# Output stores cut into multiples of 16 rows, and the last block's tiles evicted and stored one by one

## The chip, the cores and the metric

The kernel runs on one core of one Trainium2 chip. The metric is the device time of one execution in microseconds (us); the median of several runs is compared. The engines are TensorE (PE, with its weight loads PEld), VectorE (DVE), ScalarE (ACT), GpSimd (POOL) and SyncE (SP). SP does no arithmetic here: it issues nearly all DMAs, one after another in program order.

## The reference, cut to what matters

```python
X = np.fft.fft(x, axis=1)                 # x: 8 x 3008 x 256
X = np.fft.fft(X, axis=2)
h = X.real.reshape(24064, 256)
gate = np.maximum(h @ w_gate, 0.0)        # 256 x 1536
val = h @ w_val
out = (gate * val) @ w_out                # 1536 x 256, out: 24064 x 256 float32
```

A real part of a two-dimensional Fourier transform of each of eight batches, then a gated two-layer network on its rows.

## The kernel before, in words

The eight batches are eight blocks `b`. The transform along the sequence is a matmul with sine and cosine tables; the transform along the channels is folded into the network's weights (WA, WB, WM). Because the transform is symmetric, one set of columns gives two output rows: the rows that belong to +k and to −k. Block 0 is worked in four segments of 376 or 377 columns, blocks 1 to 7 in three thirds of 512, 512 and 481 columns. For each third, twelve tiles `fi` of 128 hidden channels are made: gate and value are computed in PSUM, multiplied by VectorE (L620), and stand in bf16 tiles `h` of 2n columns, the plus rows first and the mirrored minus rows behind them.

The output matmuls of a third (L511, `todo_out`) run while the next third's hidden tiles are made, some of them after each step. `out_steps` lays them out. It cuts the 2n columns of `h` into units of 128; each unit takes 12 matmuls of 128 x 256 into a PSUM tile `o`, and two units share one tile (two tiles `o` exist). When a pair is done, `fin` copies it with ScalarE (L518) into an SBUF tile `os` (four of them) and SP stores it. The 66 columns of a 481-column third that don't fill a unit are copied by a DMA into `LB` (L615); when 128 of them have come together they form a unit of their own, and in the last block the last 78 form one.

Neighbouring columns of a unit are output rows two apart, but a unit can cross from one run of rows to another. So `fin` walks over the rows and issues one store for each run (L528):

```python
while r[p] is not None and e < len(r) and r[e] == r[e - 1] + 2:
    e += 1
```

A unit of 128 rows thus becomes one store of 128 rows, or two such as 104 and 24, 97 and 31, 89 and 38. A row is 256 float32, 1 KB. DMAs on SP take turns on eight completion semaphores, so each also waits for the landing of the eighth before it.

Evictions are not issued at once but put into a list (`evict`), from which one is taken per tile while the blocks overlap (`paired`). After the last block's tiles nothing overlaps any more: the code calls `finish(pending)` and then `run(todo_out, len(todo_out))`, which issues the 96 output matmuls of the last third and empties the list. That last third has seven units of 128 (units 0 to 6) and the 78-row unit, in four pairs: rows 104 + 24 and 128; 128 and 97 + 31; 128 and 128; 89 + 38 and 12 + 66. For the last pair, whose second unit is shorter than 128, each unit is copied by itself (L521).

The order of instructions on each engine is the program's (a manual schedule); the tile pools insert the waits.

Of the kernel before, what the change touches and what calls it, by code (L numbers as in the profile page):

```python
# [13 lines left out]
ALU = mybir.AluOpType  # L14
# [13 lines left out]
def dram(ap, offset, pattern):  # L28
    return bass.AP(ap.tensor, offset, [list(p) for p in pattern])
# [3 lines left out]
def kernel(  # L33
# [8 lines left out]
    nc = tc.nc  # L42
    B, S, D = x.shape
    DF = moe_w_gate.shape[1]
    NF = DF // 128
# [15 lines left out]
    def single(name, shape, dt=F32, pool=const):  # L61
        return pool.tile(shape, dt, name=name, tag=name)
# [145 lines left out]
    for r, want in enumerate((0, H // 2)):  # L208
        have = H - 1 - 256 - 120 - r * H // 2
        nc.vector.scalar_tensor_tensor(gf[:, r:r + 1], in0=z[:], scalar=float(want - have), in1=gf[:, r:r + 1],  # L210
                                       op0=ALU.mult, op1=ALU.add)
# [48 lines left out]
    for n, c in enumerate(order):  # L260
        q, m = (single(f"{s}{c}", [128, NJ], pool=st_) for s in "qm")
# [41 lines left out]
    for t in range(3):  # L303
        p, ts = slice(0, ROWS[1][t]), slice(t, t + 1)
# [56 lines left out]
    def flush():  # L361
        for todo in (evict, sums):
            while todo:
                todo.pop(0)()
# [106 lines left out]
    def row_of(col, plus):  # L471

        seg, j = (3, col - 3 * NJ) if col >= 3 * NJ else divmod(col, NJ)
        if seg == 0:
            return 2 * j + 1 if plus else S - 2 * j - 1
        if seg == 1:
            return H + 2 * j + 1 if plus else H - 2 * j - 1
        if seg == 2:
            return H + 2 * j if plus else (H - 2 * j if j else None)
        return 2 * j if plus else (S - 2 * j if j else None)  # L480

    def out_steps(b, block, hs):

        nonlocal left_done
        c0, n = block

        r = [row_of(c0 + i, True) for i in range(n)] + [row_of(c0 + n - 1 - i, False) for i in range(n)]
        r = [None if v is None else b * S + v for v in r]
        units, whole = [], n // 64
        if n < 481:  # L490
            whole = 6
        for k in range(whole):
            h0 = min(128 * k, 2 * n - 128)
            units.append((lambda f, h0=h0: hs[f][:, h0:h0 + 128], [None] * (128 * k - h0) + r[128 * k:h0 + 128]))
        if n == 481:
            left_rows.extend(r[128 * whole:])
            while len(left_rows) - left_done >= 128 or b == B - 1 and left_done < len(left_rows):
                o = left_done
                k = min(128, len(left_rows) - o)
                units.append((lambda f, o=o, k=k: LB[:, f, o % 256:o % 256 + k], left_rows[o:o + k]))  # L500
                left_done += k
        steps = []
        for k in range(0, len(units), 2):
            st = {}
            some = units[k:k + 2]
            for q, (lhs, r) in enumerate(some):
                for f in range(NF):
                    def mm(st=st, q=q, f=f, lhs=lhs, m=len(r)):
                        if "p" not in st:
                            st["p"] = psO.tile([128, 2, D], F32, name="o", tag="o")  # L510
                        nc.tensor.matmul(st["p"][0:m, q, :], lhsT=lhs(f), rhs=wo[:, f, :],  # L511
                                         start=(f == 0), stop=(f == NF - 1))
                    steps.append(mm)

            def fin(st=st, some=some):
                os_ = rp.tile([128, 2, D], F32, name="os", tag="os", bufs=4)
                if len(some[-1][1]) == 128:
                    nc.scalar.copy(os_[:, 0:len(some)], st["p"][:, 0:len(some)])  # L518
                for q, (_, r) in enumerate(some):
                    if len(some[-1][1]) < 128:  # L520
                        nc.scalar.copy(os_[0:len(r), q], st["p"][0:len(r), q])  # L521
                    p = 0
                    while p < len(r):
                        e = p + 1
                        while r[p] is not None and e < len(r) and r[e] == r[e - 1] + 2:
                            e += 1
                        if r[p] is not None:
                            nc.sync.dma_start(out=dram(out, r[p] * D, [[2 * D, e - p], [1, D]]), in_=os_[p:e, q, :])  # L528
                        p = e
            last = steps[-1]  # L530

            def last_and_fin(last=last, fin=fin):
                last()
                evict.append(fin)
            steps[-1] = last_and_fin
        return steps
# [21 lines left out]
    todo_out, todo_dft, todo_fold = [], [], []  # L558
# [3 lines left out]
    def run(todo, n):  # L562
        for _ in range(min(n, len(todo))):
            todo.pop(0)()
        if not paired:
            flush()
# [61 lines left out]
    def finish(st):  # L628
        mirror(st["v"], st, 1)
        second(st)  # L630
# [10 lines left out]
    def tile_of(block, fi, uvc):  # L641
        c0, n = block
        cols = slice(c0, c0 + n)
        return {"n": n, "fi": fi, "f": slice(fi * 128, (fi + 1) * 128), "us": uvc[0][:, cols], "vs": uvc[1][:, cols], "c": uvc[2][:, cols]}
# [127 lines left out]
    for b in range(B):  # L772
# [4 lines left out]
        for blk, block in enumerate(blocks):  # L777
# [35 lines left out]
            if (b, blk) == (0, 0):  # L813
                for fi in range(NF):
                    st = tile_of(block, fi, (U, V, CB))
# [4 lines left out]
            elif not paired:  # L820
                for fi in range(NF):
                    st = tile_of(block, fi, (U, V, CB))
# [21 lines left out]
            if blk == len(blocks) - 1 or (b, blk) == (0, 1):  # L844
                run(todo_dft, len(todo_dft))
            todo_out = out_steps(b, block, hs)
        if b:
            run_fold(99)
# [1 line left out]
            U, V, CB = Un, Vn, CBn  # L850
    paired = False
    finish(pending)
    run(todo_out, len(todo_out))
# [1 line left out]
_INS = ['x', 'moe_w_gate', 'moe_w_val', 'moe_w_out']  # L855
_OUTS = [((24064, 256), 'float32')]
# [25 lines left out]
```

## Time and profile before

| | us |
|---|---|
| median of 3 runs | 652.28 (651.86 to 652.97) |
| profiled execution, whole time | 651.86 |
| profiled execution, span from first to last instruction | 650.1 |
| mean granted TensorE clock | 0.993 of full speed |
| last hidden-tile matmul begins | 628.50 |
| last output matmul and last eviction end | 639.35 and 640.07 |
| last store issued | 642.82 |

The span is what the profile shows between the first and the last instruction; the whole time holds 1.76 us more. In the lines of the profile, a name such as L511 is the kernel's line, "SPq" is an instruction of SP's queue (a DMA's issue, not its transfer), and "x4" a merged group of four. The view of windows gives for each stretch the busy time of PE, PEld, DVE, ACT and POOL with the number of instructions, then the granted TensorE clock, the mean busy share of the 16 DMA engines and the GB/s they moved. The view of waits gives: who waited, for whom, us in total, times, longest.

### The profile page before, as it was taken

The numbers are of one execution on the slowest core, as the hardware profiler recorded it, in microseconds if no ns is written. First come the engines' busy times: TensorE is split into PE (matmuls) and PEld (weight loads), VectorE is DVE, ScalarE is ACT, GpSimd is POOL, SyncE is SP. The second block draws the span as 40 slices with busy tenths as digits, with TensorE's granted clock in tenths as the row PEclk, the third lists the DMA queues.
The fourth block names the chain that finished last, engine by engine and source line by source line (L and its number), as shares of the span: only waits on it lengthen the run. The fifth ranks groups of instructions, "written<-read, shape, count | busy, mean of one in ns | idle before, by whom it ended". The sixth has DMA issues, their size and how long they took to land.

```text
span 650.1 us, 12382 instructions
## 1 busy us (share of the span) xinstructions
PE 615.6 (95%) x4077; PEld 398.0 (61%) x4124; DVE 543.5 (84%) x970; ACT 450.6 (69%) x823; POOL 535.4 (82%) x593
## 2 busy tenths in 40 slices
PE   0999999999999999999999999999999999999993
PEld 0356676566666666666666666666666666666662
DVE  8875566887889899888898898898899899999960
ACT  8697666767767677677677676777677777777731
POOL 8599997899999999999999999998966666666630
PEclk9999999999999999999999999999999999999997
DMA  8922544224340433242331434211221122111121
GB/s 227 204 67 64 177 133 131 64 63 145 95 120 22 146 109 85 74 132 64 94 94 43 134 95 104 69 48 50 61 59 35 41 70 60 51 37 50 54 66 53
DMA packets 56631, 56.69 MB, mean 87 GB/s; under 512 B 19344, under 2 KB 46544, under 8 KB 56567
## 3 DMA queue, kind: packets, MB, share of 16 engines
q1 hardware_dynamic: 48743, 40.65, 21.2%
q0 software_dynamic: 7536, 14.72, 9.2%
q8 instruction: 32, 0.52, 0.3%
q10 hardware_dynamic: 288, 0.52, 0.2%
q14 instruction: 32, 0.26, 0.1%
HBM read 32.14 MB, written 24.67 MB: 87 GB/s over the span
## 4 chain that ended last, share of the span: by engine, by line
PE 86%; DVE 6%; POOL 3%; issue 2%; ACT 1%; DVEq 0%; ACTq 0%; POOLq 0%
PE o L511 35%; PE v L586 9%; PE v L590 9%; PE v L585 7%; PE g L715 7%; PE p L722 7%; PE d L385 4%; POOL r L727 1%; DVE h L620 1%; PE p L590 1%; PE p L586 1%; PE p L585 1%; DVE h L609 1%; PE d L443 1%; ACT r L600 1%
## 5 line engine op out<-in xcount | busy, mean ns | idle before, releaser
L727 POOL TENSOR_TENSOR r<-r 128x512 f32<-128x512 f32 (+1 forms) x234 | 291.7, 1253 | 71.5 <-DVE r L726 70.0
L620 DVE SCALAR_TENSOR_TENSOR h<-r,v 128x512 bf16<-128x512 f32 (+1 forms) x468 | 297.2, 673 | 49.2 <-PE v L590 35.4
L511 PE MATMUL o<-wo,h 128*128 128x256 bf16 x2220 | 331.7, 272 | 0.0
L511 PEld LDWEIGHTS <-h 128*128 128x128 bf16 x2220 | 216.8, 98 | 112.2 <-issue 2.3
L710 ACT ACTIVATE p<-CB,b 128x512 f32<-128x512 bf16 (+1 forms) x234 | 160.1, 684 | 55.8 <-DVE r L726 54.7
L718 ACT COPY r<-g 128x512 f32<-128x512 f32 (+1 forms) x234 | 135.3, 578 | 56.5 <-PE g L715 49.1
L726 DVE SCALAR_TENSOR_TENSOR r<-r,p 128x512 f32<-128x512 f32 (+1 forms) x234 | 156.7, 669 | 0.6 <-ACT r L718 0.6
L590 PE MATMUL v<-V,WM 128*128 128x512 bf16 (+3 forms) x296 | 108.6, 367 | 2.2 <-DVE h L620 0.9
L586 PE MATMUL v<-V,WB 128*128 128x512 bf16 (+3 forms) x296 | 108.6, 367 | 2.0
L585 PE MATMUL v<-U,WA 128*128 128x512 bf16 (+3 forms) x258 | 94.2, 365 | 0.1
L609 DVE TENSOR_TENSOR h<-r,v 128x376 bf16<-128x376 f32 (+3 forms) x124 | 68.9, 581 | 25.7 <-PE v L590 13.6
L715 PE MATMUL g<-V,WM 128*128 128x512 bf16 (+1 forms) x234 | 87.8, 375 | 0.5 <-ACT r L718 0.3
L722 PE MATMUL p<-U,WA 128*128 128x512 bf16 (+1 forms) x227 | 85.1, 375 | 0.0
L518 ACT COPY os<-o 128x512 f32<-128x512 f32 x95 | 54.5, 573 | 12.4 <-PE o L511 8.1
L585 PEld LDWEIGHTS <-WA 128*128 128x128 bf16 x366 | 35.7, 98 | 40.0 <-issue 11.3
L586 PEld LDWEIGHTS <-WB 128*128 128x128 bf16 x366 | 35.7, 98 | 35.7 <-ACT WB L291 0.7
L102 POOL DMA_INDIRECT XG<-in_x_dram,gidx x48 | 48.8, 1018 | 8.6 <-issue 6.0
L113 POOL TENSOR_TENSOR XG<-XG,XD 128x510 f32<-128x510 f32 x42 | 52.5, 1264 | 0.1
L600 ACT ACTIVATE r<-g 128x512 f32<-128x512 f32 (+3 forms) x48 | 27.3, 569 | 34.9 <-PE g L586 29.8
L600 ACT ACTIVATE r<-p 128x376 f32<-128x376 f32 (+1 forms) x80 | 38.3, 491 | 18.6 <-PE p L590 10.9
L121 POOL TENSOR_TENSOR PQ<-XG 128x510 f32<-128x510 f32 x42 | 45.1, 1092 | 0.0
L590 PEld LDWEIGHTS <-WM 128*128 128x128 bf16 x366 | 35.8, 98 | 11.5 <-issue 0.2
(130 smaller groups left out, 442.1 us busy)
## 6 DMA issues: line engine op xcount, KB each, us to landing
out_dram<-os SPq DMA_DIRECT2D x128, 128.0 KB
XD<-in_x_dram SPq DMA_DIRECT2D x30, 256.0 KB
XD<-in_x_dram SPq DMA_DIRECT2D x16, 240.0 KB
CB<-ch SPq DMA_DIRECT2D x7, 376.2 KB
out_dram<-os SPq DMA_DIRECT2D x17, 120.0 KB
out_dram<-os SPq DMA_DIRECT2D x16, 112.0 KB
LB<-h SPq DMA_DIRECT2D x72, 16.5 KB
XG<-in_x_dram,gidx POOLq DMA_INDIRECT x48, 3.8
```

The source lines that it names most:

```text
L511: nc.tensor.matmul(st["p"][0:m, q, :], lhsT=lhs(f), rhs=wo[:, f, :], start=(f == 0), stop=(f == NF - 1))
L585: nc.tensor.matmul(bank[:, 0:st["n"]], lhsT=WA[i][:, st["f"]], rhs=st["us"], start=True, stop=False)
L586: nc.tensor.matmul(bank[:, 0:st["n"]], lhsT=WB[i][:, st["f"]], rhs=st["vs"], start=False, stop=True)
L590: nc.tensor.matmul(bank[:, 0:st["n"]], lhsT=WM[i][:, st["f"]], rhs=st["vs"], start=False, stop=True, skip_group_check=True)
L609: nc.vector.tensor_tensor(half_h(st, sign), (r or st["r"])[:, 0:n], st["v"][:, 0:n], op=ALU.mult)
L620: nc.vector.scalar_tensor_tensor(half_h(st, sign), in0=st["s"][1 + sign][:, 0:n], scalar=0.0, in1=st["v"][:, 0:n], op0=ALU.max, op1=ALU.mult)
L710: nc.scalar.activation(st["p"][:, 0:st["n"]], st["c"], ACTF.Copy, scale=b2[:, st["fi"]:st["fi"] + 1])
L715: nc.tensor.matmul(st["g"][:, 0:n], lhsT=WM[0][:, st["f"]], rhs=st["vs"], start=True, stop=True)
L718: nc.scalar.copy(q[:, 0:n], st["g"][:, 0:n])
L722: nc.tensor.matmul(st["p"][:, 0:n], lhsT=WA[0][:, st["f"]], rhs=st["us"], start=False, stop=True, skip_group_check=True)
L726: nc.vector.scalar_tensor_tensor(sp[:, 0:n], in0=q[:, 0:n], scalar=-0.5, in1=st["p"][:, 0:n], op0=ALU.mult, op1=ALU.add)
L727: nc.gpsimd.tensor_tensor(sm[:, 0:n], sp[:, 0:n], q[:, 0:n], op=ALU.add)
```

## The change

Two things are edited, both in `out_steps`, with one line at the end of the kernel. First, for all blocks, a run of more than 16 rows is cut: the store takes the largest multiple of 16 rows, and what is left becomes the next store, so that 97 rows become 96 and 1, and 89 become 80 and 9. Second, for the last third of the last block, each unit has a PSUM tile, an eviction and an `os` tile of its own; unit 1 (128 rows in one run) is moved to the end of the list, behind the 78-row unit, and its eviction is cut in two halves of 128 columns, one on ScalarE and one on VectorE. The final `run` goes twelve matmuls at a time, and issues the evictions that are due after each twelve. The kernel's lines behind the edit move by 7 to 8 (L511 becomes L514, L528 becomes L535, L877 becomes L885).

```diff
+            if b == B - 1:
+                units.append(units.pop(1))
         steps = []
-        for k in range(0, len(units), 2):
+        single_ = b == B - 1 and n == 481
+        for k in range(0, len(units), 1 if single_ else 2):
             st = {}
-            some = units[k:k + 2]
+            some = units[k:k + 1 if single_ else k + 2]
...
             def fin(st=st, some=some):
                 os_ = rp.tile([128, 2, D], F32, name="os", tag="os", bufs=4)
-                if len(some[-1][1]) == 128:
-                    nc.scalar.copy(os_[:, 0:len(some)], st["p"][:, 0:len(some)])
+                m = len(some[-1][1])
+                if single_ and some[0] is units[-1]:
+                    nc.scalar.copy(os_[0:m, 0, 0:128], st["p"][0:m, 0, 0:128])
+                    nc.vector.tensor_scalar(os_[0:m, 0, 128:D], st["p"][0:m, 0, 128:D], scalar1=1.0, op0=ALU.mult, scalar2=None)
+                else:
+                    nc.scalar.copy(os_[0:m, 0:len(some)], st["p"][0:m, 0:len(some)])
                 for q, (_, r) in enumerate(some):
-                    if len(some[-1][1]) < 128:
-                        nc.scalar.copy(os_[0:len(r), q], st["p"][0:len(r), q])
                     p = 0
                     while p < len(r):
                         e = p + 1
                         while r[p] is not None and e < len(r) and r[e] == r[e - 1] + 2:
                             e += 1
+                        if e - p > 16:
+                            e -= (e - p) % 16
                         if r[p] is not None:
                             nc.sync.dma_start(out=dram(out, r[p] * D, [[2 * D, e - p], [1, D]]), in_=os_[p:e, q, :])
                         p = e
...
     finish(pending)
-    run(todo_out, len(todo_out))
+    while todo_out:
+        run(todo_out, NF)
```

## The prediction

> **What bounds the kernel now.** I read the page first, section 1 for the load and section 6 for the stores, then the queue waits of SP, then the tail in the windows and the timelines.
>
> ```profile
> PE 615.6 (95%) x4077; PEld 398.0 (61%) x4124; DVE 543.5 (84%) x970; ACT 450.6 (69%) x823; POOL 535.4 (82%) x593
> ```
>
> TensorE is busy for 95% of the span, and the change takes no matmul away. What can be saved lies where TensorE is idle. The chain of waits ends like this:
>
> ```profile
> 628.86 10.49 PE o L511 x96
> 639.42 0.37 ACT os L521
> 639.80 0.27 ACTq L877
> ```
>
> The last 96 output matmuls end at 639.35 us and the last evictions at 640.07, yet the span is 650.1 us. For 10.7 us no compute engine works, and the chain does not follow what does. The waits of the SP queue name it:
>
> ```profile
> SPq L877 <- DMA out_dram<-os: 5.4, 1, 5.4
> ```
>
> The end of the program waits 5.4 us for an output store. The issues on SP in the tail (start, length):
>
> ```profile
> 635.20 0.28 SPq L528 DMA_DIRECT2D out_dram<-os  x1
> 635.52 0.74 SPq L528 DMA_DIRECT2D out_dram<-os  x1
> ...
> 639.82 0.25 SPq L528 DMA_DIRECT2D out_dram<-os  x1
> ...
> 640.12 1.70 SPq L528 DMA_DIRECT2D out_dram<-os  x1
> ...
> 641.91 0.86 SPq L528 DMA_DIRECT2D out_dram<-os  x1
> ...
> 642.82 0.34 SPq L528 DMA_DIRECT2D out_dram<-os  x1
> ```
>
> By the code and the sizes of section 6 these are the stores of 97, 31, 89, 38, 12 and 66 rows (a row is 1 KB). Now what the DMA engines do, in the last two columns (busy share of 16 engines, GB/s), behind the same stores of the block before, and in the tail:
>
> ```profile
> 576.00:579.00 3.00, 3.00 (x23) 2.02 (x22) 2.93 (x6) 2.33 (x5) 2.10 (x2) 1.00 0.07 25
> 608.60:609.60 1.00, 1.00 (x10) 0.72 (x9) 1.00 (x2) 0.71 (x2) 0.99 (x1) 1.00 0.73 250
> 645.00:648.50 3.50, 0.00 (x0) 0.00 (x0) 0.00 (x0) 0.00 (x0) 0.00 (x0) 0.50 0.07 23
> ```
>
> After 97 and 31 rows were issued at 573.2 and 573.6, a share of 0.07, about one engine of sixteen, moves 25 GB/s for microseconds; two stores of 128 rows at 607.9 and 608.3 run at ten times that. So stores of 97, 31 and 89 rows sit on one engine, one behind another. Check it: 97 + 31 + 89 rows, 19 of the 38, 16 of two 128-row stores and 7 of the last two are 259 KB, at 25 GB/s 10.4 us; from 635.8 that is 646.2, and the drain ends at 648.5 with gaps while the 38- and 12-row issues stall. The last landing in the trace is at 648.80; the span ends 1.3 us later. The tail is thus bound by one DMA engine, fed since 635.2.
>
> **The change, part by part.** The sum is made against the profiled execution, span 650.1 and time 651.86 us, so 1.76 us lie outside the span; the median of the runs, 652.28, is 0.42 above it.
>
> Multiples of 16. All large pieces (96, 80, 64, 112, 128) then have row counts of the kind that ran at 250 GB/s; the rest is at most 15 rows. A 15-row piece on one engine would be 15 KB, 0.6 us at 25 GB/s, against 89 rows and 3.6 us. This removes the one-engine queue: from the last 128-row store's landing on, nothing should be left.
>
> More issues. In the program built, SP's DMAs grow from 432 to 501, all 69 of them stores. In an undisturbed burst five stores took 584.55 to 586.52, that is 0.39 us each. Some 8 extra stores per block are 3 us of SP in about 80 us, and SP mostly waits (234 us on L518). Behind them in that queue stand the loads XD, CB and V and the copies LB. XD's last issue at the tightest place is at 70.6, POOL reads it from 85.9; CB and V are issued at 97.5 and 100.2 for a first seed at 107.5, and in later blocks over 30 us ahead. At the tightest place the lead is 7 us and one or two extra stores of 0.39 us stand ahead, elsewhere 3 us against 15 or more: zero before the tail. If that cover were gone, it would be 3 us in each of seven blocks.
>
> Single tiles. PE's order and its 96 matmuls stay, at 109 ns each, 1.31 us for a tile of 12. A tile's eviction of 256 columns takes 0.37 us (L521), so the bank of tile j is free before tile j+2 needs it. Each eviction takes one of four `os` buffers, so it also waits for the stores of four tiles before, 5.2 us earlier; a 128-row store lands 1.7 to 1.9 us after its issue (607.88 to 609.61). Covered, with little to spare for the fourth and fifth tiles. PE ends at 639.35 again.
>
> Now SP in the tail. Until 632.2 it is as before (the remaining stores of the block's second third). Then come 4 stores of tile one, 1 of tile two, 4 of tile three, 1, 1, then 4 of the 89/38 tile, 3 of the 78-row tile, and 1. The first eleven take 4.3 us at 0.39, to 636.5, or near 637 if the 16-row pieces take 0.44 (their row at 614.81). The 89/38 tile is evicted by 637.2, its four stores run to 638.8, the three of the 78-row tile (evicted 638.45) to 639.95.
>
> The last tile. Two evictions in a row, 0.64 us, become two halves side by side. ScalarE took 0.58 us for 512 columns and 0.37 for 256, so some 0.26 for 128; VectorE has no row of this kind, but 0.17 for 12 columns (L551) and 0.35 for 188 (L397) bound it; I take 0.3. The halves are ready at 639.42 + 0.3 = 639.7, just before SP is free at 639.95. So SP sets the last issue, by 0.2 us.
>
> Sum: last issue 639.95, landing 1.75 us later at 641.7, end of the span 1.3 us later: 643.0. The saving is 650.1 − 643.0 = 7.1 us; 652.28 − 7.1 = 645.2 us. Its bounds: the earliest is 639.72 + 1.7 + 1.3 = 642.7; with one more issue of 1.1 us (the 15-row store at 630.21 was such) and a landing of 2.3 us it is 644.7. So the saving is 5.4 to 7.4.
>
> One rule speaks on the small pieces. The Trainium skill, "DMA: Bandwidth & Descriptors", section "Why a DMA increments its semaphore by 16 and not by 1", says that a store uses the largest number of engines up to 16 that divides its row count; by it 15 rows use 15 engines and 9 use 9, and the remainders would cost less than my 0.6 us.
>
> **The rivals.** *SP becomes the bound.* The 15 store issues of the tail took 8.3 us in sum, 0.56 each, 0.61 with the gap. If this is their nature and not the jammed engine's doing, 22 issues from 630.21 put the last at 643.0, the end at 646.0, and the time at 648.2 us. For it: the 15-row store took 1.10 before any jam. Against: the five stores at 584.55 at 0.39.
>
> *Small stores land as late as large ones.* The stores take turns on eight semaphores, so each waits for the landing of the eighth before. The 66-row store at 642.82 landed after 6.0 us. With 5.5 us each, 22 stores take 15.1 us, last issue 644.6, landing at 650.1: no gain or within a microsecond. It decides from 3.4 us per landing on (eight times 0.42). Against: stores of 8 rows landed 1.5 us after their issue where no long store was ahead (602.50). The Trainium skill, same page, section "Rules for kernel authors", says to coalesce small transfers, since under 64 KB one pays mostly overhead; this would be its price. The trace agrees only where a long store stands ahead.
>
> *Slower: the in-order SP queue makes loads late.* The 3 us of extra issues stand ahead of XD, CB and V in each block. If POOL's folds or the seeds were waiting for them already, TensorE would stop 3 us per block: 7 × 3 = 21 us more, against 7 less, 666 us. It decides when the delay exceeds the lead, 7 us at the tightest place; PE waited for no DMA on SP's queue in this trace.
>
> That the change does not do what it says can be left aside: in the program built, the 97- and 89-row stores are 96 + 1 and 80 + 9.
>
> **How the numbers follow.** Forecast 0.80, SP as the bound 0.12, late landings 0.04, slower 0.04. A measurement of this kernel tells 0.2%, 1.3 us, from no change. Faster: 0.80 + 0.12 + 0.01 of the late landings = 0.93; same 0.03; slower 0.04. The forecast's own range is 652.28 less 7.4 to 5.4, 644.9 to 646.9; runs differed by 0.4 downwards, and the loss of the one-engine queue may free a little in other blocks, so the lower end is 644.2. The upper end takes in SP as the bound, 648.3.
>
> **What would show it.** Right: the wait of L877 (now L885) for the store falls from 5.4 to under 2 us; no stretch of share 0.07 after 641; the last issue near 640.0; span 643. Wrong in size: store issues of 0.6 us and more in the tail, or evictions that wait for stores, with gaps in the 96 matmuls. Wrong in kind: gaps of PE in the middle blocks, or an end that still waits over 4 us for a store of few rows.

## The result: 645.1 us, and the profile after

The changed kernel takes 645.1 us (median of 4 runs, 644.81 to 645.78) against 652.35 us for the kernel before (4 runs): a ratio of 0.989, 95% interval 0.9873 to 0.9907, 7.2 us less. The profiled execution has a span of 643.0 and a time of 644.81 us. On another chip the two stood at 645.04 and 652.24.

The page after shows the same work. TensorE's busy share rises because the span is shorter, and its busy time by 2.4 us because the page before lacks some matmul records (4077 of PE against 4124 of PEld; now both are 4124). Neither is a sign of other work:

```profile
PE 618.0 (96%) x4124; PEld 397.9 (62%) x4124; DVE 544.0 (85%) x971; ACT 451.1 (70%) x826; POOL 535.2 (83%) x593
```

The end of the chain of waits, the answer to the three lines before:

```profile
628.92 10.49 PE o L514 x96
639.41 0.03 ACTq L522
639.44 0.04 issue
639.48 0.28 ACT os L522
639.76 0.02 issue
639.78 0.29 DVE os L523
```

The 96 matmuls take 10.49 us as before and end at 639.41 instead of 639.35. So nothing was gained in any block ahead of the tail. What changed is the stretch from there to the end of the span: 10.7 us before, 3.6 now. The wait of the program's end for a store, from the view of SP's waits:

```profile
SPq L885 <- DMA out_dram<-os: 0.8, 1, 0.8
```

It was 5.4 us. The last issues on SP (the 12- and 64-row stores merged, the 2-row store, the last tile's 128 rows), and the DMA engines in the last windows (the last two columns are their busy share and GB/s):

```profile
638.81 0.93 SPq L535 DMA_DIRECT2D out_dram<-os  x2
...
639.78 0.43 SPq L535 DMA_DIRECT2D out_dram<-os  x1
...
640.32 0.36 SPq L535 DMA_DIRECT2D out_dram<-os  x1
```

```profile
641.00:641.60 0.60, 0.00 (x0) 0.00 (x0) 0.00 (x0) 0.00 (x0) 0.00 (x0) 1.00 0.62 213
642.00:643.00 1.00, 0.00 (x0) 0.00 (x0) 0.00 (x0) 0.00 (x0) 0.00 (x0) 1.00 0.02 8
```

The last store runs at 213 GB/s and a share of 0.62; the long stretch at a share of 0.07 is gone. The trace's landing records put its landing at 642.03, 1.71 us after its issue began.

### The profile page after: what moved, and what is told of

Read it like the earlier page. It is cut to its first block, busy times and chain, and to the rows that moved or that the text cites. A ratio compares the mean times of both kernels' runs of the same rounds, so it can differ in the third digit from the quotient of the medians.

```text
span 643.0 us, 12542 instructions
## 1 busy us (share of the span) xinstructions
PE 618.0 (96%) x4124; PEld 397.9 (62%) x4124; DVE 544.0 (85%) x971; ACT 451.1 (70%) x826; POOL 535.2 (83%) x593
## 4 chain that ended last, share of the span: by engine, by line
PE 87%; DVE 6%; POOL 3%; issue 2%; ACT 2%; DVEq 0%; ACTq 0%; POOLq 0%
PE o L514 35%; PE v L597 9%; PE v L592 9%; PE v L593 9%; PE g L722 7%; PE p L729 7%; PE d L385 4%; POOL r L734 1%; DVE h L627 1%; PE p L597 1%; DVE h L616 1%; PE p L593 1%; PE p L592 1%; ACT r L607 1%; PE d L443 1%
## 5 line engine op out<-in xcount | busy, mean ns | idle before, releaser
L514 PE MATMUL o<-wo,h 128*128 128x256 bf16 x2220 | 331.8, 272 | 0.0
L514 PEld LDWEIGHTS <-h 128*128 128x128 bf16 x2220 | 216.8, 98 | 112.2 <-issue 2.3
L592 PE MATMUL v<-U,WA 128*128 128x512 bf16 (+3 forms) x296 | 108.6, 367 | 0.1
L616 DVE TENSOR_TENSOR h<-r,v 128x376 bf16<-128x376 f32 (+3 forms) x124 | 68.9, 581 | 25.7 <-PE v L597 13.6
L729 PE MATMUL p<-U,WA 128*128 128x512 bf16 (+1 forms) x234 | 87.7, 375 | 0.0
L525 ACT COPY os<-o 128x512 f32<-128x512 f32 (+2 forms) x99 | 55.3, 558 | 12.6 <-PE o L514 8.3
```

Source lines behind the costliest of these rows:

```text
L592: nc.tensor.matmul(bank[:, 0:st["n"]], lhsT=WA[i][:, st["f"]], rhs=st["us"], start=True, stop=False)
L616: nc.vector.tensor_tensor(half_h(st, sign), (r or st["r"])[:, 0:n], st["v"][:, 0:n], op=ALU.mult)
L729: nc.tensor.matmul(st["p"][:, 0:n], lhsT=WA[0][:, st["f"]], rhs=st["us"], start=False, stop=True, skip_group_check=True)
```

## Experiments

To compare tails across runs I use the time from the end of the last output matmul to the end of the span, since the head of a run varies by some 0.5 us: 10.7 us before, 3.6 after.

**Which part brings it.** The cut alone (`if e - p > 16: e -= (e - p) % 16` in the kernel before, units in pairs):

```diff
                         while r[p] is not None and e < len(r) and r[e] == r[e - 1] + 2:
                             e += 1
+                        if e - p > 16:
+                            e -= (e - p) % 16
```

> The kernel before with the cut at multiples of 16 alone; units stay in pairs. Theory (one DMA engine's queue bounded the tail): the queue is gone, the last pair's evictions still end at 640.07, seven stores of it follow at 0.39 us (last issue 642.2), a landing takes 1.4 to 2.0 us, the span ends 1.0 us after the last landing: span 644.8, time about 646.8 us, so the cut by itself is worth 5.5 of the 7.2 us. Rival (the gain came from evicting and storing tiles earlier): little changes, 651 to 652 us.

Measured: 647.14 us (646.99 to 647.41), against 651.92 before on that chip, ratio 0.9922 (0.9906 to 0.9939); the tail is 5.8 us. The cut alone brings 4.8 us, 0.3 us above the time expected; its last store is issued at 642.81 instead of 642.2, 0.5 of which is the later end of the matmuls in that execution. The wait of the program's end for a store falls here too, from 5.4 to 0.5 us, with the evictions in pairs as before:

```profile
SPq L879 <- DMA out_dram<-os: 0.5, 1, 0.5
```

The rival that the earlier evictions are the gain falls as the main cause.

The other half, the changed kernel without the cut:

```diff
-                        if e - p > 16:
-                            e -= (e - p) % 16
```

> The changed kernel without the cut at multiples of 16: single tiles, unit 1 last, halves. Theory (one DMA engine's queue): the 97-row store is issued at about 633.7 instead of 635.2, the engine's 267 KB at 25 GB/s take 11.1 us, to 645.3, and with the gaps seen before up to 646.5; span 646.5 to 647.5, time 648.3 to 649.5 us. Rival (earlier evictions and stores are the gain): 645 to 645.5 us.

Measured: 650.64 us (650.49 to 651.35), ratio 0.9979 (0.9969 to 0.9988): 1.3 us, clearly less than either theory gave. The one-engine queue still sets the end. Late in it about one engine works alone (share and GB/s in the last two columns):

```profile
644.50:647.50 3.00, 0.00 (x0) 0.00 (x0) 0.00 (x0) 0.00 (x0) 0.00 (x0) 0.50 0.07 24
```

The 97-row store is issued at 634.05 instead of 635.20, 1.15 us earlier, and by the landing records the last store lands at 647.81 instead of 648.80, 1.0 us earlier. From that issue to the last landing it takes 13.8 us, as it took 13.6 before; the 11.1 us of the expectation were too few. So the single tiles alone bring little more than the earlier start of the queue. The chain of waits shows what else they do (start, length, what):

```profile
634.05 0.23 SPq L533
634.28 0.05 issue
634.33 7.13 DMA out_dram<-os
641.46 0.02 issue
641.48 0.04 ACTq L525
641.51 0.04 issue
641.55 0.31 ACT os L525
641.87 0.04 issue
641.91 0.28 ACT os L522
642.18 0.02 issue
642.21 0.29 DVE os L523
```

The 31-row store, behind the 97 rows on the same engine, lands 7.13 us after its issue; its `os` buffer is needed by the 78-row tile, four tiles later, whose eviction therefore waits until 641.55 instead of 638.2. A tile alone lasts 1.31 us on TensorE, a pair 2.62, so four buffers cover 5.2 us of landing instead of 10.5. Here this wait did not set the end: the stores behind it were issued from 641.95 to 642.73 and landed only at 647.34 to 647.81, behind the 89 and the 38 rows (646.35 and 647.16). The parts bring 4.8 and 1.3 us alone and 7.2 together, so with the cut the single tiles are worth some 2 us.

**Does the row count decide, or the number of stores?** As many stores in the tail (22, of which the first three belong to the block's second third and stay as they are), with a prime number of rows in the large pieces:

```diff
-                        if e - p > 16:
+                        if e - p > 16 and single_ and (e - p) % 16:
+                            e = p + max(v for v in (23, 29, 37, 61, 83, 89, 103) if v < e - p)
+                        elif e - p > 16:
                             e -= (e - p) % 16
```

> The changed kernel, but the 22 stores of the tail keep their number and the large pieces of cut runs are a prime number of rows there: 103+1, 23+1, 89+8, 29+2, 83+6, 37+1, 61+5 instead of 96+8, 16+8, 96+1, 16+15, 80+9, 32+6, 64+2. Theory (row counts without a common divisor with 16 engines run on one engine): 425 rows and 40 of the 128-row stores stand on one engine, some 19 us at 25 GB/s from 633: span about 653.5, time about 655 us. Rival (the size or the number of the stores is what counts): 645.1 us.

Measured: 658.03 us (657.73 to 658.2), ratio 1.0089 (1.0072 to 1.0105): with pieces a few rows off and as many stores, 13 us slower than the changed kernel and slower than the kernel before. This is 3 us more than expected, as the one-engine queue was again reckoned too short: it takes 22.3 us from the first large piece's issue at 633.00 to the last landing at 655.25. Evictions again wait for landings, now until the banks run out and TensorE stops. The view of waits:

```profile
ACT os L525 <- DMA out_dram<-os: 11.0, 2, 5.8
...
PEld L514 <- DMA out_dram<-os: 4.2, 1, 4.2
...
PE o L514 <- ACT os L525: 4.0, 1, 4.0
```

But the matmuls end at 645.23, 10 us before the last landing, so this stop is not what sets the end. The windows, while the 103-row piece is being worked off (it lands at 639.42):

```profile
637.00:639.00 2.00, 0.10 (x1) 0.00 (x0) 0.00 (x0) 0.00 (x0) 0.00 (x0) 1.00 0.08 28
```

A share of 0.08 and 28 GB/s: again little more than one engine. The landing records say it store by store. Beyond one record that comes with the end of the issue, there is one for each of the pieces of 103, 23, 89, 29, 83, 37 and 61 rows, as for the 97, 31 and 89 rows of before; in the kernel before there are 2 for 38 rows, 11 for 66 and 13 for 104, and in the changed kernel 6 for 6 rows, 9 for 9 and 15 for 15. For 128, 112, 96, 80, 64, 32 and 16 rows there are 16. The rule of the Trainium skill ("DMA: Bandwidth & Descriptors", section "Why a DMA increments its semaphore by 16 and not by 1"), that the engines are the largest number up to 16 that divides the row count, agrees with these counts and with the rows of before.

**Do extra stores cost under running matmuls?** First the cut everywhere but in the last third of the last block, in the kernel before:

```diff
+                        if e - p > 16 and not (b == B - 1 and n == 481):
+                            e -= (e - p) % 16
```

> The kernel before with the cut at multiples of 16 everywhere except in the last third of the last block. Theory: some 62 extra stores under running matmuls cost and bring nothing, 652.3 us within 0.5. Rival (the in-order SP queue delays loads, or the one-engine queue held up other blocks): more than 1 us off in either direction.

Measured: 651.61 us (651.48 to 652.2) against 651.92, ratio 0.9995 (0.9985 to 1.0005): no difference. The middle of the kernel neither pays nor gains.

Then an exaggeration, at most 32 rows in a store outside the last third, for 838 stores in all:

```diff
                         if e - p > 16:
                             e -= (e - p) % 16
+                        if not single_:
+                            e = min(e, p + 32)
```

> The changed kernel, but all stores outside the last third of the last block have at most 32 rows: 830 instead of 317 stores in all, some 180 us more of SP's issue time. Theory (SP's queue has cover in the middle): as the four or more pieces of a pair take 3 to 4 us of the 5.9 us between two evictions, no load is late and the time stays within 1 us of 645.1. Rival (the in-order queue makes XD, CB, V or LB late): several us per block, 660 us and more, with gaps of TensorE in the middle blocks.

Measured: 650.32 us (649.57 to 651.26), 5 us slower than the changed kernel, so my expectation missed. But the rival's place is wrong too. The first of the 96 output matmuls begins at 628.85, against 628.76 in the changed kernel: no time was lost before. The timeline of TensorE in the tail (start, length, form, count, idle time before it with its releaser):

```profile
628.85 6.71 PE L514 MATMUL o<-wo,h 128*128 128x256 bf16 x60
639.27 2.72 PE L514 MATMUL o<-wo,h 128*128 128x256 bf16 x12 [3.71 <-ACT os L525]
641.79 2.76 PE L514 MATMUL o<-wo,LB 128*78 128x256 bf16 x12
644.35 1.81 PE L514 MATMUL o<-wo,h 128*128 128x256 bf16 x12
```

and of SP:

```profile
630.42 2.65 SPq L624 DMA_DIRECT2D LB<-h  x3
633.17 14.05 SPq L537 DMA_DIRECT2D out_dram<-os  x28
```

SP was still busy with the small stores of the third before when the tail began: the first store of the last third is issued at 637.48 instead of 632.43, evictions wait for their buffers, TensorE for the evictions. In this execution (651.26 us) the matmuls behind the stop are slow besides: the last 36 take 6.9 us instead of 3.9, at a granted clock that fell from 1.00 to 0.50 (third value from the end):

```profile
639.30:641.90 2.60, 2.60 (x13) 1.84 (x13) 0.00 (x0) 0.37 (x1) 0.00 (x0) 0.50 0.34 104
```

The slower clock is not needed for the loss: an execution with a mean granted clock of 1.000 over the whole kernel, against 0.994 in this one, still took 649.57 us. To test where the loss arises, the same with `if b < B - 1:` in place of `if not single_:`, so that the last block is as in the changed kernel:

> The changed kernel with stores of at most 32 rows in blocks 0 to 6 alone; the last block as in the changed kernel. Theory (the loss of the kernel with 32-row stores arose in the last block, where SP came into the tail with a backlog and the copies LB were late; in the middle the extra stores are covered): 645.1 us within 0.5, though SP issues about 400 stores more. Rival (the extra stores cost in every block): 4 us more, 649.

Measured: 645.48 us (644.88 to 645.84) against 645.04 for the changed kernel on the same chip, with 790 stores. 0.4 us for 473 stores, and the ranges overlap. So the cover in the middle is real, and the price of a backlog is paid where the cover ends.

**What binds the tail now.** The last eviction in one piece instead of two halves:

```diff
-                if single_ and some[0] is units[-1]:
-                    nc.scalar.copy(os_[0:m, 0, 0:128], st["p"][0:m, 0, 0:128])
-                    nc.vector.tensor_scalar(os_[0:m, 0, 128:D], st["p"][0:m, 0, 128:D], scalar1=1.0, op0=ALU.mult, scalar2=None)
-                else:
-                    nc.scalar.copy(os_[0:m, 0:len(some)], st["p"][0:m, 0:len(some)])
+                nc.scalar.copy(os_[0:m, 0:len(some)], st["p"][0:m, 0:len(some)])
```

> The changed kernel with the last tile evicted whole by ScalarE (0.37 us) instead of in two halves. In the trace after, VectorE's half began only when ScalarE's had ended (639.78 after 639.76), so the two took 0.56 us. Theory (the halves are a loss, but SP is the bound at the end): the eviction ends 0.2 us earlier, at 639.85; SP is free at 640.21, so the last issue moves by 0.1 us at most: 645.0 us, within 0.2 of the changed kernel. Rival (the eviction is the bound): 0.2 to 0.3 us faster, 644.8.

Measured: 645.22 us (644.91 to 645.9); the tail is 3.6 us, as with the halves. The theory holds: the eviction is not the bound. Then, with this one eviction, another order of the units:

```diff
-                units.append(units.pop(1))
+                units[:] = [units[i] for i in (6, 0, 3, 2, 7, 4, 5, 1)]
```

> As with one eviction, and the last third's units in the order 6, 0, 3, 2, the 78-row unit, 4, 5, 1: those of many stores first, three whole ones last, so that SP has caught up when the last eviction ends. Theory (SP's issues are the bound): the last store is issued right behind the eviction, at 639.87 instead of 640.32: 0.45 us less, 644.6 us. Rival (the eviction or the landing is the bound): no change against the kernel with one eviction.

Measured: 645.28 us (645.05 to 645.48), tail 3.9 us. A miss: SP issues without a pause from 630.3 to 640.95, and the last store goes out at 640.55, 0.67 us after its eviction. One issue of the block's second third, 112 rows at 630.90, took 1.47 us in this execution, and SP did not catch up from it. Where SP never pauses, the sum of its issues binds and not which come last; whether the order helps without such a long issue is not shown. So, as a third variant, with one eviction and the changed kernel's order, eight of the issues taken from SP:

```diff
-nc.sync.dma_start(out=dram(out, r[p] * D, ...
+(nc.scalar if single_ and e - p < 16 else nc.sync).dma_start(out=dram(out, r[p] * D, ...
```

> As with one eviction, and the stores of fewer than 16 rows of the last third are issued by ScalarE's queue instead of SP's: 8 of the 22 leave SP. Theory (SP's issues are the bound): the last store is issued right behind the eviction, 0.3 to 0.45 us earlier, 644.6 to 644.8 us, if ScalarE's issues of some 0.35 us fit between its evictions, which leave 0.94 us. Rival: ScalarE's issues delay an eviction and with it the matmuls, 645.5 us or more.

Measured: 644.8 us (644.4 to 645.21), tail 3.1 us. As the ranges of the three overlap, the last was measured again beside the changed kernel on one chip:

> The changed kernel once more, on the same chip as the next run, for comparison: 645.1 us, and 3.6 us from the end of the last matmul to the end of the span.

> The kernel with one last eviction and the stores of fewer than 16 rows of the last third on ScalarE's queue, once more. Theory (SP's issues were the bound by 0.25 us, the serial halves cost 0.2): 3.15 us from the end of the last matmul to the end of the span against 3.6, 0.4 us faster than the changed kernel on the same chip. Rival (the difference of the single look was the chip's): within 0.1 us.

Measured: 645.04 us (644.92 to 645.11) for the changed kernel, 644.71 (644.4 to 644.8) for the variant; the ranges don't overlap, 0.33 us. Against the kernel before its ratio is 0.9884 (0.9868 to 0.9901). The last eviction and the last issue on SP there:

```profile
639.93 0.37 ACT L521 COPY os<-o 128x256 f32<-128x256 f32 x1 [0.94 <-PE o L514]
```

```profile
640.33 0.35 SPq L531 DMA_DIRECT2D out_dram<-os  x1
```

The store now follows its eviction (639.93 + 0.37 = 640.30) at once; in this execution the matmuls ended 0.5 us later than in the changed kernel's profile, so the tail is what compares: 3.1 against 3.6 us, and 3.8 for the changed kernel's second profile. This is the fastest version of the study.

## Why the prediction was right

The forecast was 645.2 us with a span of 643.0; measured were 645.1 and 643.0. That closeness is partly luck, since two terms were off and cancelled, and a third was off without an effect:

- *The one-engine queue.* Right. The cut alone brings 4.8 us, prime row counts bring the queue back and more, and the forecast's sign to look for, the wait for the last store falling from 5.4 to under 2 us, is there (0.8). But the reckoning of the queue's length before was short. I laid the end at 648.5 instead of 646.2 to gaps while the 38- and 12-row issues stall; the trace shows DMA packets without a pause from 635.65 to 648.42, and during the stall of the 38 rows the engine keeps its rate (the 31 rows land 1.31 us behind the 97). The 97-row store by itself landed 6.1 us after its issue, at 573.24 as at 635.20, where 97 KB at 25 GB/s are 3.9 us. What the rest is stays open. The forecast does not use this length, but two expectations above missed by it. And of the 10.7 us that I called empty of compute, ScalarE's evictions fill the first 0.7, until 640.07.
- *More issues, hidden.* Right, at zero: 651.61 against 651.92 with the cut outside the tail alone. Even 473 stores more in blocks 0 to 6 cost about 0.4 us in the median, with ranges that overlap.
- *Single tiles, covered.* Right for the sum, as the matmuls take 10.49 us without a gap. But I called the cover "with little to spare" and did not work out what lies on its other side: it stands on the cut, as the 7.13 us landing without it shows, and on an SP without a backlog, as the 32-row stores show.
- *SP in the tail.* Right that SP sets the last issue. It was predicted for 639.95 and came at 640.32. The term that was too small is the cost of an issue. SP pauses for the last time until the 89/38 tile is evicted; from there, 637.26, seven stores with the gaps behind them take 3.06 us, 0.44 each, where I put 0.39. I had that from five stores at 584.55 and called them undisturbed, but an 89-row store leads them, and they landed 5.4 to 6.1 us after their issue. Without the gaps, the 22 issues took 0.40 us each in the mean, those five 0.36 and the jammed tail 0.55. One of the 22, 112 rows at 630.87, took 0.99, but SP had caught up from it before 637. The rival in which SP's issues keep 0.56 us falls: the long issues stood behind one-engine stores and come back with them (3.01 us without the cut, 3.77 with prime pieces). Only the one near 630, which spoke for the rival, stays.
- *The halves.* Mis-sized. They do not run side by side: VectorE's half begins at 639.78, ScalarE's ended at 639.76. The trace shows VectorE waiting for ScalarE's half there; in the second profile of the changed kernel and in that of the kernel without the cut it also begins only when that half has ended, 0.03 us behind it. The evictions end at 640.07, as before the change, and not at 639.7. It cost nothing, because SP was free only at 640.21.
- *Landing and end.* 1.71 us instead of 1.75, and 1.0 us from the last landing to the end of the span instead of 1.3. At the program's end SP waits for its semaphores one after another, 0.06 us apart: behind that of the last store six more stood before (648.88 to 649.18), and one stands after (642.13). Most of the 0.37 us lost at the issue is won back here, which I had not foreseen.
- *Small stores land as late as large ones.* Wrong as a rival: the 6- to 9-row stores of the changed kernel land 1.3 to 1.5 us after their issue in the tail, the 128-row stores after 1.7 to 1.8. The advice of the Trainium skill ("DMA: Bandwidth & Descriptors", section "Rules for kernel authors") is to coalesce small transfers; 473 more, smaller stores in blocks 0 to 6 cost about 0.4 us in the median here, while SP kept up.
- *Slower, by late loads.* Not seen with the change. The mechanism of an in-order queue with a backlog exists, as the 32-row stores show, yet at the tail's evictions and not at XD, CB or V.

## What to carry to other kernels

When the chain of waits ends well before the span does, read the queue's own waits and the DMA share window by window: a share near 1/16 (0.07 here, at 25 GB/s) is one engine working off a queue, and the row counts of the stores say which put it there. Cut stores so that the large part has a multiple of 16 rows; under running work the extra issues are free as long as the queue catches up, and at the end of the program they are paid at 0.44 us each. Before making tiles smaller, multiply the number of buffers by the new time per tile and compare it with the longest landing; where the landing is longer, evictions wait (without the cut) and then TensorE (prime pieces, 32-row stores).

## What the hardware showed unexpectedly

A store issued behind a one-engine store can hold SP itself: in the kernel with prime pieces an 8-row store behind 103, 23 and 89 rows took 3.77 us to issue, until 639.47, and the 103-row store landed at 639.42; without the cut, the 38-row store took 3.01 us. In the profile of before, 38 rows took 1.70. How much an engine's queue takes before the issue stalls was not measured.

In every profile, DMA packets of 16 KB on the queue that section 3 of the page calls instruction come some 20 us apart and take 0.9 to 1.7 us. One of them begins between 629.98 and 631.06 in each of the 13 profiles; there a store's or a copy's issue takes 1.0 to 1.5 us instead of 0.4 to 0.55, and the copy LB lands after 2.3 to 3.3 us instead of 1.7. That the one causes the other is a reading of the coincidence; it was not tried.
